# A tuned attention and mixer kernel: first loads gated anew by head groups, and the last two slabs of batch 0's second mixing done by row tiles

## The chip, the cores and the metric

The kernel runs on one core of one Trainium2 chip. The metric is the time of one execution in microseconds (us) on the device. Most executions of one kernel agree within 0.3 to 0.5%, so an effect of 1% has to be measured in several rounds against the kernel before on the same chip. The "span" of a profile runs from its first to its last instruction; it is some 1.8 us shorter than the time of the same run.

## The reference, cut to what matters

Eight batches of eight heads, 576 positions and 64 values per head go through a linear attention. Its result, laid out as 576 rows of 512 values, goes through two mixings, first over positions and then over channels.

```python
phi = lambda x: np.where(x > 0, x, np.exp(x) - 1.0) + 1.0     # in the reference: phi(q), phi(k)
kv  = einsum('bhsd,bhse->bhde', phi(k), v)                    # one 64 x 64 matrix per head
num, den = phi(q) @ kv, phi(q) @ sum_s phi(k) + 1e-6
x   = num / den                                               # 8 x 576 x 512
u   = x + (relu(x^T @ w_tok1) @ w_tok2)^T                     # first mixing, over positions
out = u + relu(u @ w_ch1) @ w_ch2                             # second mixing, over channels
# float32 in and out; w_tok1 576x256, w_tok2 256x576, w_ch1 512x1536, w_ch2 1536x512
```

## The kernel before

The kernel keeps all weights in the core's memory in bf16 and works on the batches in pairs. The order of instructions on each engine is fixed by the program. Three parts matter.

**The loads.** q, k and v come in two halves of four heads each ("head groups"), 576 KB a half. SyncE issues most of them on queue q1. v of batch 0 and all weights are cast from float32 to bf16 on the way; GpSimd issues them, on queue q0. A load can be given a gate: it is issued only when another load has landed. Here what follows a gated load on its issuing engine is held back with it: in the profile of before, GpSimd stands 3.23 us ahead of v of group 1, which waits for q, issues it at 6.27 us and the weights behind it, which have no gate, from 7.37 us on.

```python
def load(nm, n, c, gate=None):            # q, k or v of batch n, head group c: SyncE, queue q1
    ...
    return after(nc.sync.dma_start(...), gate)
def load_v0(c, gate=None):                # v of batch 0, cast: GpSimd, queue q0
    ...
load("k", 0, 0)
q_in = load("q", 0, 0)
load_v0(0)
load("q", 0, 1)
load("k", 0, 1)
...
load_v0(1, q_in)                          # GpSimd waits here until q of group 0 has landed
...                                       # then on the same GpSimd queue: w1, w1t, w2
c_in = [load_wc1(i) for i in range(NB)]   # four blocks of w_ch1 (L611)
c2_in = [load_wc2(0)]                     # first of four blocks of w_ch2 (L616)
for kt, t0, t1 in ((0, 0, 4), (1, 0, 4), (0, 4, T)):
    w2_put(kt, t0, t1, pool)              # reorder w_tok2 into w2p, on GpSimd
...
for c in range(2):                        # batch 1; SyncE waits for the first block of w_ch1
    for nm in "kqv":
        landed[nm + "1", c] = load(nm, 1, c, c_in[0] if nm == "k" and c == 0 else None)
c2_in += [after(load_wc2(i), landed["v1", 0] if i == 1 else None) for i in range(1, NB)]
for nm in "qkv":                          # batch 2 waits for the second block of w_ch2
    for c in range(2):
        load(nm, 2, c, c2_in[1] if nm == "q" and c == 0 else None)
```

**The big matmuls of batch 0.** `mm3` (L493) multiplies by w_ch1 and `m4_0` (L519) by w_ch2. L519 runs in twelve steps of four matmuls. Each step uses one slab of 128 rows of w_ch2 and adds into four row tiles, each with a bank of its own. The first three steps need the first block of w_ch2, the fourth needs the second block. The front end of batch 1 (phi, kv, normalising, first mixing) is threaded between these steps.

**Padding.** `warm` (L579) issues matmuls on zeros while TensorE would wait. It is meant to keep the clock up: in the profile of before TensorE waited 2.70 us, to 10.49 us, and the granted clock from 10.5 to 14.0 us was 0.52.

## Time and profile before

| | before |
|---|---|
| time, median of 3 runs before the prediction | 267.69 us (266.76 to 267.88) |
| span of the profiled run, and its mean clock | 266.2 us, 0.994 |
| TensorE busy | 96% |
| first big matmul (L493) starts | 24.14 us |
| first L519 matmul starts | 37.15 us |
| transposes of the tail rows (L471) start | 59.69 us |

The profiled run of before took 268.04 us, above the three runs in the table; a gap between two profiles can therefore be larger than the gap between the medians.

Two more views of before are wanted for the comparison. The first is the timeline of GpSimd, as start, length, engine, line, what it issues, and in brackets what its idle time before was a wait for. It shows v of group 1 issued at 6.27 us, and the first three w_ch1 blocks from 9.84 us.

```profile
6.27 1.10 POOL L116 DMA_DIRECT2D cr<-in_v_dram  x1 [3.23 <-DMA q_raw<-in_q_dram]
...
9.84 2.29 POOL L611 DMA_DIRECT2D wc<-in_moe_w_ch_dram  x3
```

The second is the queues in the first 40 us (packets, MB, share of the engines' time). q0's transfers cast, so they read twice what this view counts: 576 KB are read for the 288 KB of a half of v. Reads are therefore q1 plus twice q0: 5.93 + 2 × 4.35 = 14.63 MB.

```profile
q0 software_dynamic: 5210, 4.35, 68.8%
q1 hardware_dynamic: 2734, 5.93, 41.1%
```

### The profile page before, as it was taken

How to read it: one execution, taken by the hardware profiler on the slowest of the kernel's cores; microseconds unless marked ns; L12 is line 12 of the kernel's file. 1: busy time of each engine (PE TensorE's matmuls, PEld its weight loads, DVE VectorE, ACT ScalarE, POOL GpSimd, SP SyncE). 2: the span in 40 equal slices, each digit the busy share in tenths (PEclk: the TensorE clock that was granted, in tenths of full speed). 3: DMA queues.
4: the chain of work that ended last, by engine and by line, in shares of the span. 5: the costliest groups of instructions: out<-in, count | busy, mean ns of one | idle time of the engine just before them, and what ended most of it. 6: DMA issues, size and time to landing. Idle time of an engine off the chain costs nothing.

```text
span 266.2 us, 5085 instructions
## 1 busy us (share of the span) xinstructions
PE 254.8 (96%) x2080; PEld 133.4 (50%) x2080; DVE 144.6 (54%) x286; ACT 132.5 (50%) x211; POOL 32.6 (12%) x57
## 2 busy tenths in 40 slices
PE   7589999989999999999999999999999999999994
PEld 2466355544754454445464454445564554444642
DVE  4386655776685665866574285847564282520122
ACT  4373784429656167716773258525871354026300
POOL 3860200011001300020001300030001300000000
PEclk9799999999999999999999999999999999999999
DMA  7999999339908992489998990662055500840043
GB/s 240 256 202 287 360 202 396 139 89 304 382 8 167 253 381 101 91 199 342 407 390 193 312 374 11 137 145 66 0 118 130 121 1 0 140 118 0 2 97 100
DMA packets 50087, 48.34 MB, mean 182 GB/s; under 512 B 30288, under 2 KB 35536, under 8 KB 50064
## 3 DMA queue, kind: packets, MB, share of 16 engines
q1 hardware_dynamic: 41904, 35.53, 44.1%
q0 software_dynamic: 7440, 11.44, 19.7%
q10 hardware_dynamic: 720, 1.05, 1.2%
q8 instruction: 16, 0.26, 0.4%
q14 instruction: 7, 0.06, 0.1%
HBM read 35.85 MB, written 9.44 MB: 170 GB/s over the span
## 4 chain that ended last, share of the span: by engine, by line
PE 89%; DVE 4%; DMA 3%; issue 1%; ACT 1%; POOL 0%; DVEq 0%; POOLq 0%
PE h_ps L519 33%; PE c_ps L493 31%; PE a_ps L247 5%; PE c_ps L507 4%; PE h_ps L270 4%; DMA cr<-in_v_dram 3%; PE nd_ps L209 3%; PE kv_ps L168 2%; PE h_ps L556 1%; PE bank L430 1%; PE a_ps L258 1%; DVE o_sb L536 1%; PE h_ps L291 1%; DVE qp L139 1%; DVE x L221 1%
## 5 line engine op out<-in xcount | busy, mean ns | idle before, releaser
L493 PE MATMUL c_ps<-uT,wc 128*128 128x512 bf16 x384 | 92.1, 379 | 0.9 <-DVE ut L278 0.7
L500 ACT ACTIVATE cr<-c_ps 128x512 bf16<-128x512 f32 x92 | 54.0, 599 | 78.0 <-PE c_ps L493 78.0
L519 PE MATMUL h_ps<-wc,cr 128*128 128x512 bf16 x372 | 85.0, 379 | 0.0
L519 PEld LDWEIGHTS <-cr 128*128 128x128 bf16 x372 | 35.7, 98 | 41.0 <-issue 1.2
L493 PEld LDWEIGHTS <-wc 128*128 128x128 bf16 x384 | 35.6, 98 | 37.8 <-issue 2.9
L536 DVE TENSOR_TENSOR o_sb<-h_ps,u 128x512 f32<-128x512 f32 x31 | 21.1, 689 | 24.2 <-PE h_ps L519 24.1
L541 POOL DMA_DIRECT2D out_dram<-o_sb x24 | 14.5, 607 | 155.6 <-DVE o_sb L536 155.6
L221 DVE TENSOR_TENSOR x<-nd_ps,den 128x512 bf16<-128x512 f32 (+1 forms) x42 | 25.3, 602 | 1.4
L139 DVE TENSOR_TENSOR qp<-e,y 128x1152 bf16<-128x1152 bf16 x16 | 12.1, 758 | 15.2 <-ACT e L125 14.7
L218 DVE TENSOR_SCALAR den<-nd_ps 128x8 f32<-128x8 f32 (+1 forms) x42 | 6.8, 163 | 24.3 <-PE nd_ps L209 23.7
L125 ACT ACTIVATE e<-k_raw 128x1152 bf16<-128x1152 f32 x16 | 18.7, 1168 | 2.4 <-DMA k_raw<-in_k_dram 2.4
L282 DVE TENSOR_TENSOR u<-h_ps,x 128x1024 bf16<-128x1024 f32 x12 | 14.7, 1222 | 9.2 <-PE h_ps L270 9.2
L125 ACT ACTIVATE e<-q_raw 128x1152 bf16<-128x1152 f32 x16 | 18.4, 1159 | 0.2 <-DMA q_raw<-in_q_dram 0.2
L139 DVE TENSOR_TENSOR kp<-e,y 128x1152 bf16<-128x1152 bf16 x16 | 12.4, 776 | 8.2 <-ACT e L125 7.3
L209 PEld LDWEIGHTS <-qT 128*128 128x128 bf16 x140 | 11.3, 98 | 9.4 <-ACT qT L186 0.4
L209 PE MATMUL nd_ps<-kvbd,qT 128*128 128x130 bf16 x140 | 15.1, 223 | 0.0
L150 ACT CAST vs<-v_raw 128x1152 bf16<-128x1152 f32 x13 | 15.0, 1156 | 0.0
L131 DVE TENSOR_SCALAR y<-k_raw 128x1152 bf16<-128x1152 f32 x16 | 12.3, 769 | 2.0 <-DMA k_raw<-in_k_dram 2.0
L546 DVE TENSOR_TENSOR o_sb<-h_ps,ut 128x512 f32<-128x512 f32 x4 | 2.8, 692 | 19.1 <-PE h_ps L519 19.1
L270 PE MATMUL h_ps<-ar,w2p 128*128 128x512 bf16 x48 | 12.3, 379 | 0.0
L247 PE MATMUL a_ps<-x,w 128*128 128x512 bf16 x48 | 12.3, 379 | 0.0
L507 PE MATMUL c_ps<-uTt,wc 128*128 128x128 bf16 x192 | 12.0, 219 | 0.0
(108 smaller groups left out, 207.2 us busy)
## 6 DMA issues: line engine op xcount, KB each, us to landing
k_raw<-in_k_dram SPq DMA_DIRECT2D x16, 576.0 KB, 9.9
q_raw<-in_q_dram SPq DMA_DIRECT2D x16, 576.0 KB, 7.8
v_raw<-in_v_dram SPq DMA_DIRECT2D x14, 576.0 KB, 11.5
out_dram<-o_sb POOLq DMA_DIRECT2D x24, 256.0 KB, 4.7
wc<-in_moe_w_ch_dram POOLq DMA_DIRECT2D x8, 384.0 KB, 8.7
out_dram<-o_sb SPq DMA_DIRECT2D x9, 128.0 KB, 2.3
out_dram<-o_sb ACTq DMA_DIRECT2D x7, 128.0 KB, 2.6
out_dram<-o_sb POOLq DMA_DIRECT2D x6, 128.0 KB, 5.9
```

The lines of the kernel that those rows point to most:

```text
L125: nc.scalar.activation(out=e, in_=f, func=AF.Exp)
L139: nc.vector.tensor_tensor(out=dst.transpose([0, 2, 1, 3]), in0=e.rearrange("p (i t d) -> p i t d", i=nj, t=T), in1=y.rearrange("p (i t d) ...
L150: copy(out=vs[:, js, :, 0:D], in_=raw["v", n % 2][:, js].rearrange("p j (t d) -> p j t d", t=T))
L209: nc.tensor.matmul(out=o[:, a], lhsT=qT[b][:, t0:t0 + 128], rhs=kvbd[b][:, c, a], start=True, stop=True)
L221: nc.vector.tensor_tensor(out=x[b][:, rs[0]:rs[0] + m, HG * D * g:HG * D * (g + 1)].rearrange("p r (h d) -> p r h d", h=HG), in0=v_[:, :, ...
L247: nc.tensor.matmul(out=ps[:, mt], lhsT=w1t[:, b, ms] if r == R else w1[:, r, ms], rhs=x[b][:, r, :], start=(r == 0), stop=(r == R))
L270: nc.tensor.matmul(out=ps[:, i], lhsT=w2v(kt, r, b), rhs=ar[b][:, kt, :], start=(kt == 0), stop=(kt == NT - 1 and not add))
L493: nc.tensor.matmul(out=ps, lhsT=wc1[:, kj, 128 * mc:128 * mc + 128], rhs=uT[b][:, :, kj], start=(kj == 0), stop=(kj == NDM - 1))
L500: nc.scalar.activation(out=cr[b][:, mc, :], in_=ps, func=AF.Relu)
L507: nc.tensor.matmul(out=ps[:, m], lhsT=wc1[:, kj, 128 * mc:128 * mc + 128], rhs=uTt[:, kj, :], start=(kj == 0), stop=(kj == NDM - 1))
L519: nc.tensor.matmul(out=ps, lhsT=crt[:, kc, :] if t == 8 else cr[b][:, kc, 128 * r:128 * r + 128], rhs=wc2[:, kc, :], start=(kc == 0), stop ...
L536: nc.vector.tensor_tensor(out=o, in0=ps, in1=u[b][:, r, :], op=ALU.add)
```

## The change

It has two parts. **Part 1** is meant to bring v of the first head group sooner, since TensorE waits for it: q and k of the second group are held until k of the first has landed, v of the second until v of the first has landed. The fourth block of w_ch1 moves behind GpSimd's copies into w2p, and k of batch 1's second half is held for that block. **Part 2** ends the twelve steps of L519 after ten. The last two slabs are then done row tile by row tile, so that the four banks come free one pair after the other and not all at the end. Around it batch 1's front end is reordered, and one of its copies (`utr`, second half) moves from VectorE to ScalarE.

```diff
-    load("k", 0, 0)
-    q_in = load("q", 0, 0)
+    k_in = load("k", 0, 0)
+    load("q", 0, 0)
     make_identity(nc, identity)
-    load_v0(0)
-    load("q", 0, 1)
+    v_in = load_v0(0)                     # load_v0 now returns the instruction
+    load("q", 0, 1, k_in)
     load("k", 0, 1)
 ...
-    load_v0(1, q_in)
+    load_v0(1, v_in)
 ...
-    c_in = [load_wc1(i) for i in range(NB)]
+    c_in = [load_wc1(i) for i in range(3)]
+    for kt, t0, t1 in ((0, 0, 4), (1, 0, 4), (0, 4, T)):
+        w2_put(kt, t0, t1, pool)
+    c_in.append(load_wc1(3))
 ...  (w1t's second half and the first block of w_ch2 follow; the copies stood here)
-            landed[nm + "1", c] = load(nm, 1, c, c_in[0] if nm == "k" and c == 0 else None)
+            landed[nm + "1", c] = load(nm, 1, c, c_in[3 * c] if nm == "k" else None)
 ...
+    def m4_end(t0):
+        for t in (t0, t0 + 1):
+            mm4(0, t, [NCH - 2, NCH - 1], wait=True)
 ...
-        [lambda kc=kc: m4_0(kc) for kc in range(NCH)]
+        [lambda kc=kc: m4_0(kc) for kc in range(NCH - 2)] + \
+        [lambda t=t: m4_end(t) for t in range(0, R, 2)]
 ...
+    at(18, mm2_half, 1, 0)
     at(18, nd, 1, 1, [0, 1])
-    at(18, mm2_half, 1, 0)
 ...
-    at(20, utr, 1, [0])
+    at(20, phi, "q", 2, 1)
+    at(21, utr, 1, [0])
     at(21, mm1_half, 1, 1)
-    at(21, phi, "q", 2, 1)
 ...
+    at(22, mm4_end, 0, 0)
+    at(22, mm4_end, 0, 1)
     at(22, mm2_half, 1, 1)
-    at(23, mm4_end, 0, 0)
-    at(23, mm4_end, 0, 1)
-    at(23, utr, 1, [1], dve)
     at(23, mm2, 1, [R])
     at(23, mm4_end, 0, 2)
+    at(23, utr, 1, [1])
     at(23, mm4_end, 0, 3)
```

More of the change, by code (lines that the diff above doesn't have):

```diff
@@ L115, in load_v0 @@
         js = slice(2 * c, 2 * c + 2)
-        after(nc.gpsimd.dma_start(out=v0[:, js].rearrange("p j t d -> p j (t d)"),
-                                  in_=src_[:, js]), gate)
+        return after(nc.gpsimd.dma_start(out=v0[:, js].rearrange("p j t d -> p j (t d)"),
+                                         in_=src_[:, js]), gate)
     live = {}
@@ L624 @@
     nc.gpsimd.dma_start(out=w2, in_=moe_w_tok2.rearrange("(k p) s -> p k s", p=128))
-    c_in = [load_wc1(i) for i in range(NB)]
+    dve, act, pool = nc.vector.tensor_copy, nc.scalar.copy, nc.gpsimd.tensor_copy
+    c_in = [load_wc1(i) for i in range(3)]
+    for kt, t0, t1 in ((0, 0, 4), (1, 0, 4), (0, 4, T)):
+        w2_put(kt, t0, t1, pool)
+    c_in.append(load_wc1(3))
     nc.gpsimd.dma_start(out=w1t[half[1], 1, :], in_=w1r[:, 2 * R])
     c2_in = [load_wc2(0)]
-    dve, act, pool = nc.vector.tensor_copy, nc.scalar.copy, nc.gpsimd.tensor_copy
-    for kt, t0, t1 in ((0, 0, 4), (1, 0, 4), (0, 4, T)):
-        w2_put(kt, t0, t1, pool)
     w_ = bank()
```

## The prediction

> **What bounds the kernel now.** I read first the page: shares, the forty slices, the chain of waits. Then I read the chain in order of time, the busy time by stretches, the DMA queues in short windows, and last the timeline of VectorE where the second edit works.
>
> ```profile
> PE 254.8 (96%) x2080; PEld 133.4 (50%) x2080; DVE 144.6 (54%) x286; ACT 132.5 (50%) x211; POOL 32.6 (12%) x57
> PEclk9799999999999999999999999999999999999999
> ...
> PE 89%; DVE 4%; DMA 3%; issue 1%; ACT 1%; POOL 0%; DVEq 0%; POOLq 0%
> ```
>
> TensorE is the bound: busy 96% and 89% of the chain. The gain can only come from stretches where it waits, runs at a lower clock or does padding ("warm" matmuls, L579). The stretches (start:end, length, then busy PE, PEld, DVE, ACT, POOL, clock, DMA) say where these are:
>
> ```profile
> 7.80:10.50 2.70, 0.01 (x2) 0.03 (x3) 0.29 (x1) 0.00 (x0) 2.70 (x5) 1.00 1.11 313
> 10.50:14.00 3.50, 3.50 (x65) 3.07 (x65) 1.61 (x5) 2.29 (x5) 2.65 (x5) 0.52 1.31 198
> 14.00:24.10 10.10, 8.61 (x127) 6.76 (x126) 8.77 (x16) 6.12 (x19) 3.50 (x5) 1.00 1.26 233
> 24.10:45.80 21.70, 21.67 (x198) 10.96 (x197) 12.19 (x25) 14.64 (x24) 2.28 (x3) 1.00 1.10 314
> 45.80:60.10 14.30, 12.49 (x90) 7.41 (x90) 11.01 (x22) 5.16 (x7) 1.24 (x2) 1.00 0.41 134
> 60.10:266.00 205.90, 202.23 (x1590) 102.44 (x1588) 106.70 (x206) 100.17 (x152) 16.43 (x28) 1.00 0.57 164
> ```
>
> TensorE is idle from 7.80 to 10.49, then runs 3.5 us at half clock, is gappy until 24.1, full until 45.8, and gappy again until 60.1. Both edits sit in the two gappy places. After 60.1 it is full. The chain names what it waits for:
>
> ```profile
> 1.47 8.98 DMA cr<-in_v_dram
> 10.49 0.63 PE bank L369 x36
> 11.12 1.08 PE bank L179 x9
> ...
> 15.72 1.06 DVE kp L139
> ...
> 24.14 1.02 PE c_ps L493 x4
> ...
> 54.61 0.76 DVE qp L139
> 55.37 0.60 DVE u L314
> 55.97 1.20 DVE o_sb L536 x2
> 57.16 0.60 DVE uT L328
> ```
>
> The start hangs on v of batch 0, first head group, which takes 8.98 us from issue to landing. Its queue, q0, in 4.0–5.4 us and then in 5.4–9.4 us (packets, MB, share):
>
> ```profile
> q1 hardware_dynamic: 256, 0.56, 109.4%
> ...
> q1 hardware_dynamic: 419, 0.92, 65.7%
> q0 software_dynamic: 262, 0.29, 41.9%
> ```
>
> In the first window q0 has no line: k and q of group 0 go first. In the second v's 0.29 MB share the engines with q and k of group 1, which nothing needs before 12.2 us (L131 on q, then ACT's exp of k at 13.78).
>
> [...] v does cast (576 KB read, 288 KB written)[...]; gating the others is the way to favour it. [...] after 2.7 us of idling the clock is 0.52 for the next 3.5 us.
>
> **Part 1, loads.** q of group 1 now waits for k of group 0 to land (used at 4.60 us), k of group 1 follows it, and v of group 1 waits for v of group 0. By 5.4 us q1 has just finished its first two loads in either kernel. q of group 1 is issued at 4.65 instead of 1.76. A load issued by SP behind a filled q0 took 3.5 us to its first packet at 17.4 us, 1.0 us at the start on empty queues; so I put its start at 6.5–7. v then has the engines to itself from 5.4. Alone, q0 moves about 0.2 MB/us (202 GB/s between 10 and 20 us), so 0.29 MB take 1.5 us and some 0.6–0.9 us to land: 7.5–7.8 instead of 10.45. TensorE is busy with padding until 7.8 anyway, so kv begins at 7.8–8.0 instead of 10.49: 2.6 us.
>
> More comes from the clock: without 2.7 us of idling, the half-clock stretch should go. Its chain holds kv (0.63, against 0.45 for the same 36 matmuls at 17.2), nine transposes (1.08, against 0.68 at 14.7), and two padding matmuls (1.17, against 0.65): 1.2 us, of which ACT's copies hide a part. I count 0.9. After that VectorE and ACT set the pace (exp of q 1.17, exp of k 1.15, y 0.75, min 0.75), with q landing at about 9 and k at 10.5, both ahead of use. kp moves from 15.72 to about 12.4. v of group 1 flows in 9.9–11.5 as before, because q0 was not free earlier in the old order, so it lands at about 12.2 against a new need of 13.5. The mixing weights land at 14–15.4 as before, against needs of 15.3 (w1) and 17.7 (w2p after two POOL copies, about 17.0). Sum: 3.5 us, all still there at the first big matmul (24.14 to about 20.6), if every weight keeps its slack.
>
> Charged against it: the second quarter of the second weights (L616) is issued only when v of batch 1 lands, 31.0 us, and lands at 37.1, when SP's queue goes on. Its first use, the fourth step of the channel output, is at 40.1 now and would be at 36.6. The landing hardly moves, since q0 and q1 are full from 10 to 34 us. I charge 0.5 us. Moving the fourth weight block behind the POOL copies costs nothing: it would land at about 27, needed at 31.
>
> **Part 2, end of the first second mixing.** No instruction goes, except that one of two 128x1024 copies moves from VectorE (0.68) to ACT (1.01). The matmul work between 45.8 and 60.1 is unchanged. By starts of matmuls against 512 columns/0.216 us, 3.2 us of this stretch are waits; the largest are 0.89 and 0.29 at 57.4–59.3 (banks held by outputs that VectorE has not yet added), 0.50 at 46.8 (a small bank held by the normalising multiply), 0.41 at 49.8 and 0.37 at 55.6. Reordered, the u half goes before the normalising ones, both exps run early, slabs 0 and 1 get their last two steps before u's second half, and their additions lie beside it. Walking the new order with the old durations, VectorE is nearly full: 0.69 (u), 3 normalisings of 1.1, 1.1 and 0.8, four phi pieces 3.0, two additions 1.3, u 0.68, ut 0.69, addition 0.65 is 10.0 us from about 47.0, so the last bank comes free at 57.3. TensorE waits some 0.35 behind the first u and 0.65 before the last transposes. The big matmuls of batch 1 (30 of them from 60.08) start at about 58.1: 2.0 us. I keep 1.6, as such walks run short.
>
> Sum: 3.5 − 0.5 + 1.6 = 4.6 us. All later work is full TensorE, so it passes to the end: 267.69 − 4.6 = 263.1 us.
>
> **Rivals.** (a) v gains only 1.4 us: if q of group 1 gets its first packets already at 5.7, the queues share as before and v lands near 9. For it: at the start SP's first packet came 1.0 us after issue. Against it: every issue behind a full other queue waited 2–3.5 us. Then part 1 is about 2 us with the clock: 265. (b) A later wait eats it: a weight or a load of batch 1, gated on landings whose times don't move, becomes the bound. For it: L616 above, and ACT's cast of v at 33.88, which would want 30.4 while v lands at 31.0. Against it: all the others have 1 us or more. Then 264.5–265.5. (c) Part 2 gains nothing, since VectorE remains the chain there (11.01 of 14.30 busy): 264.7. (d) All goes right and nothing is charged: 3.5 + 2.0 gives 262.2, so over 2% (below 262.3) needs everything.
>
> **Range.** 263.1 us; 261.7 to 265.2. The ceiling of (d) lies just at the 2% line, so faster by over 2% gets 0.25; within 2% 0.74; slower 0.01, as no added work is in sight.
>
> **What would show it.** Landing of the first v at 7.5–8 (9 would be rival a); no half-clock stretch after 8 us; first big matmul (L493) near 20.6; a wait of PE at the fourth step of L519 near 36.6 of 0–1 us (more is rival b); L493 of batch 1 running in one piece from a point 5 us before 60.1. I am wrong if the first big matmul comes earlier yet the point at 60.1 does not move.

## The result, and the profile after

The changed kernel took 265.37 us (median of 4 runs, 264.96 to 265.56) against 267.26 us (median of 4 runs, 266.76 to 267.88) for the kernel before on the same chip. The ratio is 0.9926, with a 95% interval of 0.9897 to 0.9955: 0.7% faster, so within 2%. Ratios are the mean time of one kernel's fast runs over the mean of the other's in the same rounds, so they are not quite the ratio of the quoted medians. The prediction was 263.1 us, and its range ended at 265.2, so the result lies outside it, on the slow side.

The page of the changed kernel begins like this: shares and counts, the granted clock in forty slices, and the chain of what ended last.

```profile
PE 252.8 (96%) x2080; PEld 131.7 (50%) x2080; DVE 143.7 (55%) x285; ACT 134.0 (51%) x212; POOL 32.2 (12%) x57
PEclk9999999999999999999999999999999999999999
...
PE 80%; DMA 12%; DVE 4%; POOL 1%; issue 1%; ACT 0%; SPq 0%; POOLq 0%; DVEq 0%; ACTq 0%
```

The chain's share of transfers has grown from 3% to 12%: TensorE is still the engine that does the work, but its start is now hung on loads. The stretches, cut as the prediction cut them, show where:

```profile
7.80:10.50 2.70, 2.30 (x65) 1.89 (x65) 1.22 (x3) 1.58 (x4) 2.10 (x4) 1.00 1.04 358
10.50:14.00 3.50, 2.36 (x32) 1.47 (x29) 3.36 (x8) 2.88 (x6) 3.50 (x5) 1.00 1.19 165
14.00:24.10 10.10, 9.27 (x118) 6.53 (x119) 6.88 (x13) 4.95 (x17) 4.38 (x7) 1.00 1.24 205
24.10:45.80 21.70, 20.00 (x187) 10.29 (x186) 11.20 (x22) 14.36 (x23) 2.29 (x3) 1.00 1.08 289
45.80:60.10 14.30, 13.92 (x97) 8.11 (x96) 11.54 (x23) 9.03 (x13) 2.44 (x4) 1.00 0.81 235
60.10:263.60 203.50, 199.36 (x1576) 101.03 (x1574) 105.44 (x204) 97.19 (x148) 15.23 (x26) 1.00 0.57 164
```

The idle time at 7.8 to 10.5 us is gone (2.30 us busy against 0.01), and so is the half clock that followed it (1.00 against 0.52). The stretch at 45.8 to 60.1 is fuller (13.92 against 12.49). But the stretch from 24.1 to 45.8, where TensorE had been busy for 21.67 of 21.70 us, is now busy for 20.00 only. The chain in order of time says what it waits for there (start, length, engine or transfer, line):

```profile
1.47 6.64 DMA cr<-in_v_dram
...
8.40 0.73 POOL cr L116
...
11.79 7.69 DMA wc<-in_moe_w_ch_dram
...
19.90 10.48 DMA q_raw<-in_q_dram
...
30.47 1.17 ACT e L125
31.67 0.77 DVE qp L139
32.48 0.68 PE tp L179 x9
```

Read it from the top. v of group 0 lands at about 8.1 us. That landing lets GpSimd issue v of group 1 (L116) at 8.40 us, and behind it the weights, from 9.13 us on. The first block of w_ch1, issued at 11.79 us, lands at 19.48 us. It is the gate of batch 1's loads, whose q lands at 30.4 us. Then exp, min and the transposes follow, and TensorE has nothing in between. The waits from 24 to 42 us show the loads behind it (engine, line, what it waits for: us in total, times, longest):

```profile
ACT e L125 <- DMA k_raw<-in_k_dram: 2.4, 1, 2.4
...
PE tp L179 <- DVE qp L139: 1.0, 1, 1.0
PE c_ps L493 <- ACT cr L500: 0.7, 1, 0.7
```

ScalarE stands 2.4 us for k of batch 1, whose exp begins at 27.85 us. Behind it come the outputs of L493 (from 28.92 us), whose banks TensorE wants back (the 0.7), and later q's phi (from 30.47 us; the 1.0). None of these three waits was in that window of the kernel before. The waits of this view are rounded; the two gaps of TensorE last from 28.48 to 29.55 and from 31.10 to 32.48 us.

The timeline of GpSimd in the changed kernel, as shown of before:

```profile
8.40 0.73 POOL L116 DMA_DIRECT2D cr<-in_v_dram  x1 [5.37 <-DMA cr<-in_v_dram]
...
11.79 2.65 POOL L611 DMA_DIRECT2D wc<-in_moe_w_ch_dram  x3
```

The wait ahead of L116 is now for v of group 0 (5.37 us) and no longer for q (3.23 us), and everything after it is issued about 2 us later. The queues in the first 40 us:

```profile
q0 software_dynamic: 4732, 3.88, 65.3%
q1 hardware_dynamic: 2720, 5.90, 40.8%
```

They have read 5.90 + 2 × 3.88 = 13.66 MB, 0.97 MB less than before. At the rate of before, about 14.63 MB in the 38 us from the first packets on or 0.39 MB/us, that is 2.5 us of loading. The landings agree (us; issue plus the time to landing, which the view rounds to 0.1 us, so they are good to 0.05; the last column is the first experiment that puts one gate back, told below):

| transfer | before | the change | v1_early |
|---|---|---|---|
| v of batch 0, group 0 | 10.47 | 8.07 | 7.67 |
| v of batch 0, group 1: issued | 6.27 | 8.40 | 6.18 |
| v of batch 0, group 1: landed | 12.67 | 13.90 | 12.68 |
| w_tok2 | 15.43 | 16.97 | 15.66 |
| w_ch1, first block | 17.44 | 19.48 | 17.98 |
| k of batch 1, first half | 24.53 | 27.79 | 24.83 |
| q of batch 1, first half | 27.04 | 30.40 | 27.54 |
| v of batch 1, first half | 30.93 | 33.29 | 30.43 |
| w_ch2, second block | 36.97 | 39.41 | 37.17 |

Only the first row is earlier in the change. The milestones of TensorE tell the same in three steps. The first big matmul starts at 21.37 instead of 24.14 us (2.77 us gained). The first L519 matmul starts at 36.34 instead of 37.15 us (0.81 us left). The tail transposes start at 56.66 instead of 59.69 us (3.03 us, so part 2 added about 2.2).

### The profile page after: what moved, and what is told of

The parts are those of the page before. It is cut to its first block, busy times and chain, and to the rows that moved or that the text cites.

```text
span 263.6 us, 5086 instructions
## 1 busy us (share of the span) xinstructions
PE 252.8 (96%) x2080; PEld 131.7 (50%) x2080; DVE 143.7 (55%) x285; ACT 134.0 (51%) x212; POOL 32.2 (12%) x57
## 4 chain that ended last, share of the span: by engine, by line
PE 80%; DMA 12%; DVE 4%; POOL 1%; issue 1%; ACT 0%; SPq 0%; POOLq 0%; DVEq 0%; ACTq 0%
PE h_ps L519 31%; PE c_ps L493 29%; PE a_ps L247 5%; PE c_ps L507 4%; DMA q_raw<-in_q_dram 4%; PE h_ps L270 4%; DMA wc<-in_moe_w_ch_dram 3%; PE nd_ps L209 3%; DMA cr<-in_v_dram 3%; DMA uT<-u 2%; PE kv_ps L168 2%; PE h_ps L556 1%; DVE qp L139 1%; DVE o_sb L536 1%; DVE x L221 1%; PE h_ps L291 1%
## 5 line engine op out<-in xcount | busy, mean ns | idle before, releaser
L493 PE MATMUL c_ps<-uT,wc 128*128 128x512 bf16 x384 | 92.2, 379 | 1.0 <-ACT cr L500 0.7
L519 PE MATMUL h_ps<-wc,cr 128*128 128x512 bf16 x372 | 85.1, 379 | 0.0
L519 PEld LDWEIGHTS <-cr 128*128 128x128 bf16 x372 | 35.7, 98 | 41.1 <-issue 1.5
L493 PEld LDWEIGHTS <-wc 128*128 128x128 bf16 x384 | 35.5, 98 | 37.8 <-issue 3.3
L536 DVE TENSOR_TENSOR o_sb<-h_ps,u 128x512 f32<-128x512 f32 x31 | 21.1, 688 | 24.2 <-PE h_ps L519 24.1
L221 DVE TENSOR_TENSOR x<-nd_ps,den 128x512 bf16<-128x512 f32 (+1 forms) x42 | 25.3, 602 | 1.4
L125 ACT ACTIVATE e<-k_raw 128x1152 bf16<-128x1152 f32 x16 | 18.7, 1168 | 4.9 <-DMA k_raw<-in_k_dram 4.9
L209 PE MATMUL nd_ps<-kvbd,qT 128*128 128x130 bf16 x140 | 15.1, 223 | 0.2 <-ACT u L312 0.2
L131 DVE TENSOR_SCALAR y<-q_raw 128x1152 bf16<-128x1152 f32 x16 | 12.2, 763 | 0.5 <-DMA q_raw<-in_q_dram 0.5
```

Of the source, the lines that this page charges most:

```text
L125: nc.scalar.activation(out=e, in_=f, func=AF.Exp)
L131: nc.vector.tensor_scalar(out=y, in0=f, scalar1=1.0, scalar2=1.0, op0=ALU.add, op1=ALU.max)
L209: nc.tensor.matmul(out=o[:, a], lhsT=qT[b][:, t0:t0 + 128], rhs=kvbd[b][:, c, a], start=True, stop=True)
L221: nc.vector.tensor_tensor(out=x[b][:, rs[0]:rs[0] + m, HG * D * g:HG * D * (g + 1)].rearrange("p r (h d) -> p r h d", h=HG), in0=v_[:, :, ...
L493: nc.tensor.matmul(out=ps, lhsT=wc1[:, kj, 128 * mc:128 * mc + 128], rhs=uT[b][:, :, kj], start=(kj == 0), stop=(kj == NDM - 1))
L519: nc.tensor.matmul(out=ps, lhsT=crt[:, kc, :] if t == 8 else cr[b][:, kc, 128 * r:128 * r + 128], rhs=wc2[:, kc, :], start=(kc == 0), stop ...
```

## The experiments

My theory after reading the profiles was this: the gate of v of group 1 on v of group 0 stalls GpSimd's queue by 2 us, the whole stream of loads falls behind, and most of part 1's gain is eaten by the loads of batch 1; before the second call I added the second block of w_ch2 as a limit behind them. Part 2 gives most of what is seen. The rivals were: the new gate of batch 1's second half, the place of the copies, or the late gate of w_ch2's second block does it on its own; or part 1 is worth something and part 2 is not. Each call used one chip, so only kernels of one call are compared to the last half per cent. "Block 2" below is the second block of w_ch2, and the "wait at L519" is the one ahead of its fourth step, which needs that block.

### First call: each part alone, and two gates

Before took 267.36 us here (median of 7).

**p1_only**: the change with part 2 undone.

```diff
-    [lambda kc=kc: m4_0(kc) for kc in range(NCH - 2)] + [lambda t=t: m4_end(t) for t in range(0, R, 2)]
+    [lambda kc=kc: m4_0(kc) for kc in range(NCH)]
     (and the at(18) to at(23) lines as before)
```

> The edits of the loads and weights alone, the order of the first second mixing as before. My theory: of the 2.8 us gained at the first big matmul (24.14 to 21.37 in the profile of the change) 2.0 us are lost again between 28 and 33 us, because k and q of batch 1 land at about 27.8 and 30.4 instead of 24.5 and 27.0. So the first step of the channel output (L519) starts near 36.3 and the time is about 0.8 us under before, 266.5. Rival: the gain of the loads reaches the end and it is the reordering that gave nothing; then 264.5 to 265.

It took 268.15 us (267.23 to 268.64, 4 runs), ratio 1.0026 (0.9996 to 1.0056): a miss. Part 1 alone gains nothing at all, where I had still given it 0.8 us. Its first big matmul starts at 22.02 us, 2.1 us sooner than before's. Its timeline shows where that goes:

```profile
39.43 1.02 PE L519 MATMUL h_ps<-wc,cr 128*128 128x512 bf16 x4 [1.28 <-DMA wc<-in_moe_w_ch_dram]
```

TensorE stands 1.28 us for block 2, which landed at 39.34 us. (The wait is 1.45 us "by the ends of the matmuls", that is, if the last matmul is taken to end 0.216 us after its start, which is the spacing of these matmuls (before: four of L519 from 106.87 us, the next four matmuls from 107.73); the profile's modelled ends are later.) In this run k of batch 1 happened to land at 25.68 us, so TensorE didn't wait for it, and the next wait in line took the gain instead. The 0.67 us that were still left at the tail transposes (59.02 against 59.69 us) were lost behind them; 0.5 of these us are a wait near 90 us that the fourth call comes back to.

**p2_only**: the kernel before with part 2 alone.

```diff
     (the kernel before, with m4_end, the shortened list of big steps
      and the at(18) to at(23) lines of the change)
```

> The reordering at the end of the first second mixing alone, the loads as before. My theory: the start is unchanged (first big matmul at 24.1, first L519 at 37.2), and the stretch to the long run of L493 of batch 1 is 2.2 us shorter (60.08 to about 57.9), so about 2.0 to 2.2 us under before: 265.1. Rival: the reordering gives under 0.5 us by itself, 266.8 or more.

It took 264.94 us (264.32 to 265.29, 4 runs), ratio 0.9903 (0.9873 to 0.9934), as expected. Part 2, the smaller term of the prediction's sum, gives the whole result, 2.4 us here. The profiles of before and of the change show how, and that of p2_only has the same lines as the change 0.2 us later. In the timeline of TensorE of before, the first big matmuls of batch 1 stood 0.73 us for a bank that VectorE's addition of the tail rows (`ut`, L278) had not yet freed:

```profile
58.54 1.32 PE L493 MATMUL c_ps<-uT,wc 128*128 128x512 bf16 x4 [0.73 <-DVE ut L278]
```

In the change, the timeline of TensorE has the same work running on without a gap:

```profile
55.13 1.69 PE L493 MATMUL c_ps<-uT,wc 128*128 128x512 bf16 x6
56.66 0.39 PE L471 MATMUL tp<-identity,ut 128*128 128x128 bf16 x4
```

The timeline of VectorE shows why. In the kernel before, the outputs of the first two row tiles are added (L536) from 55.88 us, and a copy stands between them and the tail rows (L278):

```profile
55.88 1.28 DVE L536 TENSOR_TENSOR o_sb<-h_ps,u 128x512 f32<-128x512 f32 x2
57.08 0.68 DVE L328 COPY uT<-tp 128x1024 bf16<-128x1024 bf16 x1
57.79 0.69 DVE L278 TENSOR_TENSOR ut<-bank,x 64x512 bf16<-64x512 f32 x1
```

In the change, both are 3.0 us earlier (some 0.8 of them because L519 started sooner), and the copy is ScalarE's:

```profile
52.85 1.28 DVE L536 TENSOR_TENSOR o_sb<-h_ps,u 128x512 f32<-128x512 f32 x2
...
54.76 0.69 DVE L278 TENSOR_TENSOR ut<-bank,x 64x512 bf16<-64x512 f32 x1
```

Part 2 was only tested whole, so how much of it is the row tiles, how much the moved copy and how much the new order isn't shown.

**v1_early**: the change, but with v of group 1 gated on q of group 0 as in the kernel before.

```diff
-    load("q", 0, 0)
+    q_in = load("q", 0, 0)
-    load_v0(1, v_in)
+    load_v0(1, q_in)
```

> The change, but v of head group 1 of batch 0 is issued when q of head group 0 has landed (about 6.0 us), as before, not when v of group 0 has landed (8.1). q of group 1 still waits for k of group 0. My theory: what follows on GpSimd's queue is issued about 2 us sooner, the first weight block lands at about 17.5 to 18 instead of 19.5, k of batch 1 is issued then and lands near 25, and TensorE's waits of 0.86 and 1.17 us at 28.5 and 31.1 mostly go: 263.5 to 264.2. Rival: the bytes of v of group 1 now stand against those of q and k of group 1, which land 1 us later and delay the start by as much: 265 or more.

It took 263.77 us (263.25 to 264.45, 4 runs), ratio 0.9868 (0.9839 to 0.9897), as expected and 1.6 us below the change (on another chip). The landings are in the table above: v of group 0 is no later than in the change (7.67), and all the others are back near the times of before. By 40 us its queues have read 6.06 + 2 × 4.34 = 14.74 MB. The first big matmul starts at 20.41 us, the first L519 matmul at 33.49. What is left is a wait of 0.75 us (by the ends of the matmuls) at L519, for block 2 at 37.17 us. The fourth step of L519 starts at 37.18 us, 2.9 us before that of the kernel before (40.09). This kernel beats both.

**k1_early**: the change, but batch 1's loads are issued when w_tok2 has landed and not when the first block of w_ch1 has.

```diff
-    nc.gpsimd.dma_start(out=w2, ...)
+    w2_in = nc.gpsimd.dma_start(out=w2, ...)
-    load(nm, 1, c, c_in[3 * c] if nm == "k" else None)
+    load(nm, 1, c, (c_in[3] if c else w2_in) if nm == "k" else None)
```

> The change, but k of batch 1 waits for the second mixing weight to land (about 17.0 us) instead of the first block of the channel weights (19.5). All before it is untouched. My theory: k, q and v of batch 1 land about 2 us sooner, both waits of TensorE (0.86 and 1.17 us at 28.5 and 31.1) go: 263.5. Rival: the limit there is the shared bandwidth and not the issue; k lands hardly sooner and the weight blocks later, and the time stays at 265 or more.

It took 266.18 us (265.82 to 266.65, 4 runs), ratio 0.9958 (0.9932 to 0.9984): a miss, no faster than the change. k of batch 1 was issued 1.0 us sooner than in the change and landed at 25.3 us, but the wait only moved: block 2 landed at 40.25 us, and TensorE stood 1.32 us for it, by the ends of the matmuls. Here the load that was issued sooner made another transfer later. (A period of half clock from 15.1 us, of which more below, also put the first big matmul at 22.98 us.) k of batch 1 alone was thus not the cause; it is one of several things in that stream.

### Second call: the gate of block 2, and one gate alone

Before took 267.12 us (median of 7).

**c2_early**: the change, with block 2 gated on q of batch 1 and not on v; the third block keeps the gate on v.

```diff
-    after(load_wc2(i), landed["v1", 0] if i == 1 else None)
+    after(load_wc2(i), landed["q1", 0] if i == 1 else landed["v1", 0] if i == 2 else None)
```

> The change, but the second block of wc2 waits for q of batch 1 (first half, landed 30.4 in the profile of the change) instead of v (33.3); the third block waits for that v. My theory now: the earlier loads set two limits one behind the other, the landing of k and q of batch 1 and the landing of this block (39.4), which the fourth step of L519 waits for; in the profile of the change the first hid the second. With the second moved forward the block lands near 37 and the time is 0 to 1 us under the change, 264.4 to 265.4, by how early k and q happen to land. Rival: this block limits nothing; the time is that of the change or longer, since later loads of batch 1 share with it.

It took 265.46 us (264.89 to 265.95, 4 runs), ratio 0.9936 (0.9914 to 0.9958): just outside what I had expected, and no gain over the change. Block 2 lands at 35.54 us, and the wait for it is gone. In its place ScalarE waits for v of batch 1's second half, landed at 41.48 us, and TensorE waits for ScalarE's cast (0.78 us by the view, 0.94 by the ends of the matmuls):

```profile
42.69 0.48 PE L168 MATMUL kv_ps<-vs,kp 64*64 64x65 bf16 x36 [0.78 <-ACT vs L150]
```

**k1_c2_early**: both gates moved.

> k of batch 1 waits for the second mixing weight (as in k1_early) and the second block of wc2 for q of batch 1 (as in c2_early). My theory: the wait of 1.32 us at the fourth step of L519 in k1_early goes, which gives 264.9 or less, against 266.2 for k1_early. Rival: k1_early is slow by what its early loads do to the weights of the start (first big matmul at 22.98, not 21.37), and 266 stays.

It took 268.17 us (267.29 to 269.23, 4 runs), ratio 1.0040 (1.0004 to 1.0076): a miss, and slower than before. The second half of v landed at 43.68 us, and kv waited 2.94 us for it (by the ends of the matmuls).

**v1_c2_early**: v1_early and c2_early together.

> v of group 1 issued on q's landing (as in v1_early) and the second block of wc2 on q of batch 1. My theory: the wait of 0.75 us at the fourth step of L519 in v1_early goes: 263.0. Rival: the block takes bandwidth from k, q and v of batch 1, second half, whose use is close; 263.8 or more.

It took 264.57 us (264.10 to 266.41, 4 runs), ratio 0.9916 (0.9877 to 0.9955): also a miss, no better than v1_early. Block 2 landed at 38.23 us, so the new gate didn't bring it sooner; in this profile no wait at L519 was left all the same, as a half-clock period from 15.1 to about 18.5 us had put the first big matmul at 22.47 us. (In it four matmuls of L430 take 0.85 us from start to start, from 16.22 us; at full clock, in before from 19.56 us, they take 0.44.)

**q1_gate_only**: the kernel before with part 2 and a single gate of part 1, q of group 1 on k of group 0.

```diff
-    load("k", 0, 0)
+    k_in = load("k", 0, 0)
-    load("q", 0, 1)
+    load("q", 0, 1, k_in)
     (and part 2; all else as before)
```

> The kernel before with the reordering at the end, and of the edits of the loads only one: q of group 1 waits for k of group 0. v of group 1 is issued on q's landing, the weights and the loads of batch 1 as before. My theory: this one gate holds the whole gain of the loads (v of group 0 lands at about 7.8) and what was added beside it gave nothing or cost: 263.8 or less, as v1_early. Rival: moving the fourth weight block behind the copies, or gating k of batch 1's second half, is worth something: 264.5 or more.

It took 264.95 us (264.20 to 265.41, 4 runs), ratio 0.9913 (0.9886 to 0.9941): a miss. I had expected 263.8 or less, by comparison with v1_early of the first call on another chip. The fourth call settles it on one chip.

### Third call: less to load, and the clock

Before took 267.17 us (median of 11).

**no_c2_0**: the change without the load of w_ch2's first block, which is set to zero instead. The result is wrong (relative error 0.282); this takes 384 KB off q0 and nothing off TensorE.

```diff
-    c2_in = [load_wc2(0)]
+    nc.gpsimd.memset(wc2[:, 0:NCH // NB, :], 0.0)
+    c2_in = [None]
```

> The change, with the first block of wc2 (0.79 MB read) not loaded but set to zero by GpSimd: the result is wrong on purpose. Nothing else moves. My theory: from about 10 to 41 us the loads run as one stream near 0.39 MB/us without a pause, so leaving out 0.79 MB brings all that comes after it forward by about 2 us: v of batch 1 from 33.3 to about 31.5, the second block of wc2 from 39.4 to about 37.3, and the time by 1 to 2 us: 263.4 to 264.4. Rival: each landing follows from its gate and a fixed time of its own, not from the bytes before it; the second block still lands at 39 or later and the time is that of the change, 265.4.

It took 265.54 us (263.56 to 266.35, 4 runs), ratio 0.9929 (0.9894 to 0.9964). Block 2 landed at 36.34 us, 3.1 us sooner than in the change, and the wait at L519 was gone: the landing follows how much the stream has to carry, as the theory says. The profiled run took 263.56 us at a clock of 1.0, but the three others took 265.2 to 266.4 us at clocks of 0.991 to 0.994. The test of the landing came out as expected. The time, which I had put at 263.4 to 264.4 us, was a miss: with this wait gone, the runs at a clock below 1 gained nothing over the change. Only the run at full clock was profiled, so what bound the others isn't shown.

**v1_again** is v1_early unchanged, **v1_warm** is v1_early with one more padding matmul in each of two waits, and **v1_best** is v1_warm with v of batch 1's second half gated on the landing of k's second half, to favour block 2.

```diff
     v1_warm, in two places:
-    warm(w_, 1, 256)            -    warm(live["g", 1], 1, 256)
+    warm(w_, 2, 256)            +    warm(live["g", 1], 2, 256)
     v1_best, besides:
-    load(nm, 1, c, c_in[3 * c] if nm == "k" else None)
+    load(nm, 1, c, c_in[3 * c] if nm == "k" else landed["k1", 1] if nm + str(c) == "v1" else None)
```

> v1_early once more, as the base of the next two on the same chip: 263.8, with the first big matmul at 20.4 if the clock stays up and about 1.5 us later if a half-clock period of 3.4 us falls at 15 us, as it did in the profile of v1_c2_early (22.5). Rival: 263.8 was luck of that chip, and it is nearer 265.

> v1_early with one more padding matmul of 256 columns in each of the two waits at 11 and 13 us. My theory: the half-clock period at 15 us comes of these waits; with them filled the granted clock is 0.998 or more in all runs, and the time is 0 to 1 us under v1_again, by how many of its runs had the period. Rival: the padding stands in the way of the transposes, 0.3 us or more longer, and the clock is no other.

> v1_warm, and v of batch 1, second half, waits for k of the second half to land (about 32.3), so that the second block of wc2 has less to share with. My theory: the block lands near 36.3 instead of 37.2 and its wait of 0.75 us shrinks: 0.3 to 0.7 us under v1_warm. Rival: v of the second half lands after 38 us and ACT, which casts it, holds up the next relu: no gain or a loss.

v1_again took 263.85 us (263.20 to 264.11, 4 runs), ratio 0.9873 (0.9852 to 0.9895), which repeats the first call on another chip. v1_warm took 264.13 us (263.71 to 264.98, 6 runs), ratio 0.9894 (0.9871 to 0.9916): the clock was 0.998 or more in all six runs, and the time was no better. Whether the padding kept the clock isn't shown, as v1_again had 1.0 in three of its four runs without it; but the clock was not what bound this kernel. v1_best took 267.30 us (266.20 to 267.93, 6 runs), ratio 0.9999 (0.9975 to 1.0023). Block 2 did land at 36.17 us, but v's second half landed at 40.38 us; ScalarE stood 3.98 us for it, and kv 2.09 us (by the ends of the matmuls). A gate that favours one load took the whole gain away by delaying another.

### Fourth call: the four that decide, on one chip

Before took 266.98 us (median of 11). Each kernel has 6 runs: **same_after** is the change, **same_v1** is v1_early, **same_q1** is q1_gate_only, **same_p2** is p2_only.

> The change itself, beside the next three. My theory: it is bound by the landing of the second block of wc2 near 39.4 us or by k and q of batch 1, so about 1.9 us under before whatever its clock was; no better than the reordering alone (same_p2) within 0.5 us. Rival: its loads do give 1 us or more over same_p2.

> v1_early on the same chip. My theory: 1.3 to 1.7 us under same_after, as its stream of loads has no pause. Rival: within 0.5 us of same_after on the same chip.

> q1_gate_only on the same chip. My theory: the stream of loads is as full as in v1_early, so it lies within 0.5 us of same_v1, and what parted them before was the clock on the other chip. Rival: it lies near same_p2, and the fourth block behind the copies, or the gate on k of batch 1's second half, is what makes the loads' gain.

> The reordering alone on the same chip. My theory: 2.2 us under before, so within 0.5 us of same_after and 1 us or more above same_v1. Rival: 1 us or more above same_after.

| kernel | loads | median us (range) | ratio to before (95%) |
|---|---|---|---|
| same_p2 | as before | 265.07 (264.51 to 265.39) | 0.9923 (0.9904 to 0.9943) |
| same_after | all of part 1 | 265.06 (264.74 to 265.99) | 0.9936 (0.9913 to 0.9959) |
| same_v1 | part 1 but the gate of v of group 1 | 264.16 (262.99 to 264.55) | 0.9888 (0.9866 to 0.9909) |
| same_q1 | only the gate of q of group 1 | 264.35 (263.37 to 264.64) | 0.9892 (0.9872 to 0.9913) |

All of part 1 together is worth nothing (265.06 against 265.07 us). Undoing its one gate on v of group 1 gives 0.9 us on this chip; between the first call and the run of the result, on two chips, it was 1.6. One gate on q of group 1 alone is as good as all of v1_early, so neither the place of the copies nor the gate on batch 1's second half shows a gain.

The chain in order of time shows where the gate on v acts. In same_after:

```profile
31.66 7.72 DMA wc<-in_moe_w_ch_dram
39.38 0.04 issue
39.42 1.02 PE h_ps L519 x4
```

In same_v1:

```profile
31.55 7.40 DMA wc<-in_moe_w_ch_dram
38.95 0.04 issue
39.00 1.02 PE h_ps L519 x4
```

Both wait for block 2, and its landing sets the fourth step of L519. In the three profiles with all of part 1 (the change, p1_only, same_after) it landed at 39.4 us, although it was issued at 33.8, 31.4 and 31.7 us; in v1_early, v1_again, v1_warm and same_v1, which lack the gate, at 37.1, 38.5, 38.5 and 38.95 us. In each of the seven the step starts within 0.1 us of the landing. same_q1 has no such wait: block 2 lands there at 37.2 us and the step starts at 38.75 us, after a start slowed by a half-clock period (0.50 of the clock from 16.5 to 18.0 us).

The clock is a rival here: all six runs of same_after and of same_p2 were at 0.994 or less, while four of the six of same_v1 and of same_q1 were at 0.997 or more. The four runs of the result speak against it. Two of them were at 1.000 and took 265.36 and 265.38 us, two at 0.990 and 0.991 and took 264.96 and 265.56 us: at full clock the change is no faster.

The bytes read (MB, q1 plus twice q0) in the profiles of these kernels and of some earlier ones line up with that:

| by | before, same_p2 | the change, same_after, p1_only | v1_early, same_v1 | same_q1 |
|---|---|---|---|---|
| 18 us | 6.14, 6.22 | 5.58, 5.42, 5.62 | 6.04, 5.88 | 5.84 |
| 40 us | 14.63, 14.65 | 13.66, 13.92, 13.94 | 14.74, 14.14 | 14.60 |

The three profiles with the gate on v are 0.69 to 0.97 MB behind before at 40 us, and those without it are 0.49 MB behind (same_v1) or not at all. By 18 us, when no load of batch 1 has moved a byte in any of them, the three are already 0.5 to 0.7 MB behind, 1.3 to 1.8 us at 0.39 MB/us. The rest of the lag at 40 us comes after that; that it is partly a consequence, as loads of batch 1 and 2 wait for landings that are late, is my reading. Not shown is why the stream is slow once the new gate has opened. q0 did not stand empty for longer: its first packet of v of group 1 moved at 9.86 us in the change and at 9.71 us in v1_early, where that load was issued 2.2 us sooner. It ran slower. In the change, the queues together moved 108 to 169 GB/s from about 10.2 to 11.6 us, with v of group 1 and the first weights issued, where q0 alone moved some 200 GB/s at other times (202 from 10 to 20 us of before). From 12 to 17 us, with q0 alone, the three profiles with the gate read 1.68 to 1.78 MB; before, same_p2, v1_early, same_v1 and same_q1 read 1.96 to 2.02 MB. That the slowness goes with the gate is shown, how the late issue brings it about is not.

One more thing was seen and not settled. In the profiles of the change, p1_only, v1_early and q1_gate_only TensorE waits 0.2 to 0.6 us (1.2 us in v1_best) between 85 and 91 us for a transposing transfer of batch 2 that lands late; before, same_after and same_v1 have none of it. It is there or not in runs of the same kernel, so I ascribe it to no edit.

## Why the prediction was wrong

**What held.** v of group 0 was predicted at 7.5 to 8 us and landed at 8.07 us. q of group 1 was predicted to have its first packets at 6.5 to 7 us and had them at 6.56. The first big matmul was predicted 3.5 us earlier and came 2.77 us earlier in the first profile of the change (1.22 in that of same_after). Rival (a), in which v gains only 1.4 us, fell. Part 2 was booked at 1.6 us after a walk that gave 2.0; it measured 2.4 and 1.9 us alone (p2_only, same_p2) and 2.2 us within the profile of the change. The deduction for caution was not needed. Rival (c) fell.

**What failed** is the step on the loads behind the first: "v of group 1 flows in 9.9–11.5 as before, because q0 was not free earlier in the old order", with "The mixing weights land at 14–15.4 as before" and "The landing hardly moves, since q0 and q1 are full from 10 to 34 us. I charge 0.5 us." I asked when q0 could *move* v of group 1, and not when GpSimd could *issue* it and what stands behind it. q0 did take it up at 9.86 us, as I had said, but it did not flow "as before". With the new gate, GpSimd's queue issues it at 8.40 us instead of 6.27, and the weights behind it about 2 us later. It landed at 13.90 us where I had put 12.2, and w_tok2 at 16.97 where I had put 15.4 at the latest. Every landing behind it came later than before, by 1.1 us (the second block of w_ch1) to 3.3 us (q of batch 1), and block 2 by 2.4 us. The fullness of q0 and q1 was a fact of the old order: by the two tables of stretches, the queues moved 165 GB/s from 10.5 to 14 us in the change against 198 before, and 205 against 233 from there to 24.1 us.

The traces show what I passed over. The weights w1 have no gate, yet they are issued at 9.13 us in the change and at 7.37 us before, right behind the held load (8.40 and 6.27 us). And in k1_early and c2_early one load brought sooner left another late: in k1_early k of batch 1 landed at 25.3 us instead of 27.79, and block 2 at 40.25 instead of 39.41; in c2_early block 2 landed at 35.54 us, and v's second half at 41.48, where ScalarE began to cast it at 38.91 us in the change. That v, which casts, is best favoured by gating the other loads was my assumption; no run tested another way.

**Rival (b) was the right one**, with a wrong mechanism. It had later waits eat the gain because landings "don't move"; it gave 264.5 to 265.5 us, and the result is 265.37. The waits are the ones it names, the loads of batch 1 and L616, but those landings moved, backwards. Its place for the wait (the fourth step of L519, near 36.6 us) held in p1_only and same_after, at 39.4 us; in the first profile of the change the wait came before it, at 28.5 and 31.1 us, for k and q of batch 1.

**The terms of the sum.** Predicted: 3.5 − 0.5 + 1.6 = 4.6 us. Measured: part 1 with its charge gives 0 (same_after against same_p2), where 3.0 was booked, and part 2 gives 1.9 to 2.4, where 1.6 was. The step-by-step loss of part 1 in the change's profile is 2.77 us at the first big matmul, of which 0.81 are left at the first L519 matmul. At 39.4 us block 2 lands, and no path to L519's fourth step can pass that landing. Without part 1 that step begins at 40.09 us in the profile of before and at 39.75 us in that of same_p2, so at most 0.3 to 0.7 us of the 3.0 could pass. Without the gate on v the step began 2.9 us before that of before in v1_early, 1.5 in v1_again and 1.1 in same_v1: about the booked gain was within reach, but only when block 2 landed early (37.1 us), and why it did so in that one profile isn't shown. One sum of the prediction is also slightly off: its three differences for the clock add up to 1.1 and not 1.2 us; it booked 0.9.

**The clock.** The prediction counted 0.9 us for the half-clock period that should go. It went in the first profile of the change. In that of same_after a period of half clock stands from 15.3 to 18.7 us (0.50 from 16.5 to 18.0 us), the first big matmul starts at 22.91 us, and yet the run took 265.00 us: the landings bind either way. In v1_warm it was kept off in six runs and gained nothing that the intervals show. So that term was real on TensorE and worth nothing at the end. Nor could it be counted on: of the fifteen profiles of kernels with any of the new gates, nine have a half-clock period that begins between 8 and 17 us.

**What stays open:** what decides whether the half-clock period falls at 15 us, why k of batch 1 landed at 25.7 us in one profile and 27.8 us in another with the same order of loads, and the slow stretch of the loads noted above.

## What to carry to other kernels

Here a gate that was to favour one transfer held back everything behind it on its engine: v of group 1 was issued at 8.40 us instead of 6.27, and the weights behind it at 9.13 instead of 7.37. Follow the issue times of that whole queue to the end of the program before calling the landings "as before". With the loads one full stream (0.39 MB/us), bringing one forward made another late (block 2 at 35.54 us in c2_early, v's second half at 41.48), so ask which landing will end last. Here the one gate on the queue of q and k was worth about 0.7 us, and with all of part 1, the gate on the other queue among it, nothing was left.

## What else the traces show

- When q0 was alone (10 to 20 us of before, where q1 moved 0.04 MB), it wrote 1.96 MB, some 0.2 MB/us, and so read 0.39 MB/us. The whole stream of cast and plain loads read 0.39 MB/us too, in the 38 us from the first packets on.
- In before, SyncE's first load was issued at 0.74 us, with the queues empty, and had its first packet at 1.85 us. Behind a filled other queue it took longer: v of batch 0 (group 0), issued at 1.47 us, had its first packet at 5.5 us, k of batch 1, issued at 17.43, at 21.0, and block 2, issued at 31.47, at 33.2. These are 1.7 to 4.0 us, where the prediction has 2 to 3.5.
- v1_early and the change differ in the gate of v of group 1 alone. With it that load was issued at 8.40 instead of 6.18 us, the blocks of w_ch1, which have no gate, from 11.79 instead of 10.08, and block 2 landed at 39.41 instead of 37.17 us.
- In same_after the granted clock was 0.60 from 15.0 to 16.5 us, 0.50 from there to 18.0 and 0.76 from there to 19.5. In the 3.0 us before, TensorE was busy for 1.77 us (1.14 and 0.63 in the two halves) and waited 0.86 us at most at a time. The first profile of the same kernel had 2.36 us busy in that stretch (1.16 and 1.20), and a clock of 1.00 up to 19.5 us. How much idling brings the half clock isn't shown.
